# Loading the last weight of a decode step: one transfer with an outermost dimension of four, or four transfers of 32 partitions

## The chip, the cores and the metric

The kernel runs on one core of a Trainium2 chip. The metric is the device time in microseconds (us), median of the runs. A ratio is computed as the mean time of one kernel's fast runs over that of the other's of the same rounds, so it is not quite the ratio of the medians that are quoted.

## The reference

One decode step of two sequences: attention over a cache of 16384 positions and 32 heads, and beside it a small MLP, mixed by a gate. Cut to what matters:

```python
def _A_ref(x, k_cache, v_cache, wq, wo):          # B=2, H=32, Sk=16384, Dh=128, D=1024
    q = ...                                       # x @ wq, by heads
    p = softmax(einsum("bhqd,bhkd->bhqk", q, k_cache) * Dh ** -0.5)
    o = einsum("bhqk,bhkd->bhqd", p, v_cache)
    return o.transpose(0, 2, 1, 3).reshape(B, Sq, H * Dh) @ wo      # wo: 4096 x 1024, bf16
# _B_ref: layernorm, w1, w2, w3, w4 ... (cut)
return g * a + (1 - g) * b
```

K and V together are 537 MB, wo is 8.39 MB. wo is needed last, once the attention output of every head is there.

## The kernel before

K and V tiles of 8.39 MB (128 partitions x 64 KB) stream through three large buffers. wo takes such a buffer too, so its load is issued when the buffer of the last K tile is free. At that moment the last V tile is still in flight. SP issues all transfers.

```python
def load_v(i):
    t = big_tile("Vn")                            # [128, 32768] bf16, one of three buffers
    nc.sync.dma_start(out=t[:].rearrange("p (j d) -> p j d", d=Dh), in_=cache_rows(A_v_cache, i))
# ... (cut)
WO_SPLIT = [16, 8, 4, 2, 1, 1]                    # rows per partition in each of six pieces

def load_wo():
    t = big_tile("wo")[:].rearrange("p (r n) -> p r n", n=D)
    src = A_wo.rearrange("(h a r) n -> a h r n", a=4, r=32)
    r0 = 0
    for n in WO_SPLIT:
        nc.sync.dma_start(out=t[:, r0 : r0 + n, :], in_=src[:, :, r0 : r0 + n, :])
        r0 += n
# ... (cut)
def wo_stage():
    Q = const.tile([P, B, 32], BF16)
    for b in range(B):
        nc.vector.transpose(out=Q[:, b, :], in_=OT[:, b, :])
    wo = wt.pop("wo").rearrange("k r (p c) -> k r p c", c=KC)
    for r in range(32):
        for c in range(KC):                       # KC = 8: 256 products in all
            nc.tensor.matmul(wo_acc[:, c, :], lhsT=wo[:, r, :, c], rhs=Q[:, :, r],
                             start=(r == 0 and c == 0), stop=(r == 31 and c == KC - 1))
```

`OT` holds dimension d of head h at partition d. VectorE transposes it in blocks of 32 x 32, so partition 32a+h of `Q` holds head h, dimensions 32a to 32a+31. Partition 32a+h of wo must therefore hold wo's rows 128h+32a+r. One step in memory cannot express that order over 128 partitions; the source has two dimensions, a (4) and h (32).

## Time and profile before

| | before |
|---|---|
| time, median of the first 3 runs | 1420.8 us (1418.2 to 1423.4) |
| span of the profiled run | 1417.6 us |
| last V tile usable | 1317.0 us |
| Q ready | 1324.8 us |
| first and last piece of wo usable | 1372.7 and 1413.8 us |
| PE waiting for wo | 73.7 us |

The slices of the page divide the span into 40 equal parts: granted TensorE clock and busy share of the DMA engines in tenths, and GB/s.

```profile
PEclk9988888687886887888885878888878787888555
DMA  9999999999999999999999999999999999999221
GB/s 413 439 423 435 439 428 429 437 426 441 428 432 432 429 438 433 424 441 437 419 443 435 424 435 435 432 432 431 439 430 429 435 437 422 441 433 394 85 89 58
```

DMA is busy all the time at about 430 GB/s, except in the last three slices, where it moves 85, 89 and 58 GB/s at two and one tenths. What is loaded there shows in the timeline (start, duration, engine, line, operation, count; in brackets the idle time before it and what ended it):

```profile
1296.17 103.53 SPq L125 DMA_DIRECT2D wo<-in_A_wo_dram  x6
...
1316.97 5.65 PE L338 MATMUL O<-Vn,PT 128*32 128x512 bf16 x64 [10.20 <-DMA Vn<-in_A_v_cache_dram]
...
1324.60 0.21 DVE L374 STREAM_TRANSPOSE Q<-OT 128x32 bf16<-128x32 bf16 x1
...
1372.70 7.86 PE L378 MATMUL wo_acc<-Q,wo 128*128 128x2 bf16 x128 [48.34 <-DMA wo<-in_A_wo_dram]
...
1393.63 4.01 PE L378 MATMUL wo_acc<-Q,wo 128*128 128x2 bf16 x64 [13.07 <-DMA wo<-in_A_wo_dram]
...
1413.81 0.65 PE L378 MATMUL wo_acc<-Q,wo 128*128 128x2 bf16 x8 [2.00 <-DMA wo<-in_A_wo_dram]
...
1414.96 0.41 SPq L523 DMA_DIRECT2D out_dram<-out_pm  x1
```

The last V product starts at 1316.97 us, Q is ready at 1324.8, and then PE stands still for 48 us until the first piece of wo is there. SP needs 103 us to get six instructions out. The waits of PE in this stretch (what waited, for what, us in total, times, longest):

```profile
PE wo_acc L378 <- DMA wo<-in_A_wo_dram: 73.7, 6, 48.3
PE O L338 <- DMA Vn<-in_A_v_cache_dram: 10.2, 1, 10.2
```

PE is not the limit: the group of all 256 products is 16.4 us of work, and 73.7 us of idle time before it (busy, mean ns of one | idle time and its cause):

```profile
L378 PE MATMUL wo_acc<-Q,wo 128*128 128x2 bf16 x256 | 16.4, 199 | 73.7 <-DMA wo<-in_A_wo_dram 73.7
```

A table of stretches (limits and length in us, busy time and count of five engines, granted clock, DMA share, GB/s) shows how many DMA engines work:

```profile
core 0: us, PE busy (x) PEld busy (x) DVE busy (x) ACT busy (x) POOL busy (x), PEclk, DMA share, GB/s
1304.00:1314.00 10.00, 0.56 (x2) 0.50 (x2) 1.27 (x5) 0.78 (x2) 0.00 (x0) 0.50 0.70 237
1314.00:1324.00 10.00, 6.33 (x70) 3.16 (x71) 0.00 (x0) 0.58 (x1) 0.00 (x0) 0.65 0.25 80
...
1334.00:1344.00 10.00, 0.00 (x0) 0.00 (x0) 0.00 (x0) 0.00 (x0) 0.00 (x0) 0.50 0.26 85
1344.00:1354.00 10.00, 0.00 (x0) 0.00 (x0) 0.00 (x0) 0.00 (x0) 0.00 (x0) 0.50 0.23 79
```

A share of 0.25 at a fifth of the usual rate is four engines of 16.

The trace also has one record for each packet that a DMA engine moved, with start, size and duration, though not with the number of the engine. The 64 KB packets at the end are rows of the last V tile, and the 128 packets of 32 KB are the rows of wo's first piece. In the kernel before, nearly all 64 KB packets took 2.42 us; the exceptions are the 11 that started from 1308.6 us on, beside the first packets of wo, and took 3.0 to 4.1 us. Of wo's 128 packets, 63 took about 1.22 us and 34 about 2.42 us. Later two of the four engines at a time appear to hinder each other: two packets that start at 1341.4 us take 2.42 us each, while those that start around them take 1.22.

### The profile page before, as it was taken

Reading aid. Unit: us, or ns where it says so; the run is one execution under the profiler, and the core shown is the slowest. Engines: PE = TensorE matmul, PEld = TensorE weight load, DVE = VectorE, ACT = ScalarE, POOL = GpSimd, SP = SyncE. Lnnn points to the kernel's source line nnn. Section 1 sums busy time; section 2 is a strip of 40 time slices with the busy share of each in tenths; the row PEclk is TensorE's granted clock in tenths of the full one; section 3 lists DMA queues with packets and bytes.
Section 4 is the critical chain, followed back from the end, with each engine's and each line's share of the span. In section 5 each row is a group of like instructions: output and inputs, shape, how many; then the busy total and the mean of one; then the engine's idle time right before and its main releaser. Section 6 shows DMA issues by size and latency. Waiting matters only on the chain.

```text
span 1417.6 us, 12917 instructions
## 1 busy us (share of the span) xinstructions
PE 827.6 (58%) x5523; PEld 400.9 (28%) x5586; DVE 707.6 (50%) x862; ACT 45.5 (3%) x100; POOL 14.4 (1%) x45
## 2 busy tenths in 40 slices
PE   2575666655667655556666556666655565566122
PEld 2232322422234222222324222222222222222022
DVE  0665566555545554555662555665655554556000
ACT  0000000000000000000000000000000000000000
POOL 0000000000000000000000000000000000000000
PEclk9988888687886887888885878888878787888555
DMA  9999999999999999999999999999999999999221
GB/s 413 439 423 435 439 428 429 437 426 441 428 432 432 429 438 433 424 441 437 419 443 435 424 435 435 432 432 431 439 430 429 435 437 422 441 433 394 85 89 58
DMA packets 11474, 573.37 MB, mean 404 GB/s; under 512 B 1816, under 2 KB 1816, under 8 KB 2200
## 3 DMA queue, kind: packets, MB, share of 16 engines
q1 hardware_dynamic: 11416, 572.54, 93.9%
q8 instruction: 44, 0.72, 0.2%
q14 instruction: 14, 0.11, 0.0%
HBM read 572.53 MB, written 0.00 MB: 404 GB/s over the span
## 4 chain that ended last, share of the span: by engine, by line
PE 25%; DVE 21%; DMA 21%; another core or an unknown queue 12%; issue 11%; SPq 7%; ACT 2%; ACTq 0%; POOL 0%
DVE T L286 18%; DMA Kn<-in_A_k_cache_dram 16%; PE S L294 13%; SPq L125 7%; PE O L338 6%; DMA wt<-in_B_w_dram 4%; PE misc L430 3%; PE misc L201 2%; PE misc L348 2%; DMA wo<-in_A_wo_dram 2%; ACT Pr L322 1%; DVE PT L326 1%; ACT Os L346 1%; DVE mx L315 1%
## 5 line engine op out<-in xcount | busy, mean ns | idle before, releaser
L294 PE MATMUL S<-T,z 128*128 128x512 bf16 x1985 | 581.3, 421 | 342.3 <-DVE T L286 321.7
L286 DVE STREAM_TRANSPOSE T<-Kn 128x1024 f32<-128x1024 f32 x512 | 612.2, 1229 | 266.8 <-DMA Kn<-in_A_k_cache_dram 218.3
L294 PEld LDWEIGHTS <-z 128*128 128x128 bf16 x2048 | 218.7, 107 | 699.4 <-issue 537.2
L338 PE MATMUL O<-Vn,PT 128*32 128x512 bf16 x2048 | 119.8, 387 | 10.2 <-DMA Vn<-in_A_v_cache_dram 10.2
L338 PEld LDWEIGHTS <-PT 128*32 128x32 bf16 x2048 | 73.1, 140 | 56.2 <-issue 16.2
L365 DVE TENSOR_TENSOR OT<-misc,rinv 128x2 bf16<-128x2 f32 x32 | 5.1, 160 | 162.1 <-PE misc L348 162.1
L201 PE MATMUL misc<-rs,ones_f 128*128 128x2 f32 x64 | 17.9, 350 | 76.5 <-DVE rs L358 76.5
L378 PE MATMUL wo_acc<-Q,wo 128*128 128x2 bf16 x256 | 16.4, 199 | 73.7 <-DMA wo<-in_A_wo_dram 73.7
L346 ACT COPY Os<-O 128x512 f32<-128x512 f32 x32 | 18.7, 585 | 1092.1 <-PE O L338 1092.1
L348 PE MATMUL misc<-osel,Os 128*128 128x2 f32 x256 | 33.7, 254 | 22.2 <-ACT Os L346 22.2
L517 DVE TENSOR_TENSOR fin<-wo_acc,g_bc 128x16 f32<-128x16 f32 x1 | 0.2, 174 | 89.7 <-PE wo_acc L378 89.7
L348 PEld LDWEIGHTS misc<-osel,Os 128*128 128x128 f32 x256 | 31.0, 191 | 36.7 <-ACT Os L346 36.7
L430 PEld LDWEIGHTS <-wt 128*128 128x128 bf16 x576 | 35.7, 171 | 18.4 <-DMA wt<-in_B_w_dram 17.1
L305 DVE TENSOR_REDUCE m<-S 128x1 f32<-128x512 f32 x32 | 22.2, 693 | 36.9 <-PE S L294 36.9
L201 PEld LDWEIGHTS misc<-rs,ones_f 128*128 128x128 f32 x64 | 16.2, 314 | 81.2 <-issue 78.5
L326 DVE STREAM_TRANSPOSE PT<-Pr 128x512 bf16<-128x512 bf16 x32 | 22.7, 711 | 28.7 <-ACT Pr L322 28.7
L378 PEld LDWEIGHTS <-wo 128*128 128x128 bf16 x256 | 15.9, 169 | 74.2 <-DMA wo<-in_A_wo_dram 74.2
L322 ACT ACTIVATE Pr<-S,nb 128x512 bf16<-128x512 f32 x32 | 22.0, 687 | 124.0 <-DVE nb L317 121.0
L201 PE MATMUL misc<-mdiag,ones_f 128*128 128x128 f32 x64 | 15.6, 325 | 15.6 <-DVE mdiag L308 15.6
L315 DVE TENSOR_REDUCE mx<-misc 64x1 f32<-64x64 f32 x64 | 14.2, 222 | 19.0 <-PE misc L201 18.6
L264 POOL TENSOR_TENSOR z<-qsel,own 128x32 bf16<-128x32 bf16 x32 | 10.8, 337 | 1225.6 <-PE S L294 1194.6
L239 PE MATMUL misc<-xT,wt 128*128 128x2 bf16 x256 | 7.1, 165 | 25.5 <-DVE xT L234 23.1
(70 smaller groups left out, 106.9 us busy)
## 6 DMA issues: line engine op xcount, KB each, us to landing
wt<-in_B_w_dram SPq DMA_DIRECT2D x2, 7168.0 KB
wt<-in_B_w_dram SPq DMA_DIRECT2D x2, 2048.0 KB, 37.6
wo<-in_A_wo_dram SPq DMA_DIRECT2D x1, 4096.0 KB
wo<-in_A_wo_dram SPq DMA_DIRECT2D x1, 2048.0 KB
wo<-in_A_wo_dram SPq DMA_DIRECT2D x1, 1024.0 KB
Kn<-in_A_k_cache_dram SPq DMA_DIRECT2D x32, 52.3
Vn<-in_A_v_cache_dram SPq DMA_DIRECT2D x32, 37.9
wo<-in_A_wo_dram SPq DMA_DIRECT2D x1, 512.0 KB
```

The source lines that it names most:

```text
L125: nc.sync.dma_start(out=t[:, r0 : r0 + n, :], in_=src[:, :, r0 : r0 + n, :])
L201: nc.tensor.matmul(ps[:], lhsT=ones_f[:], rhs=src, start=True, stop=True)
L286: nc.vector.transpose(out=T[:].rearrange("p w j s -> p j w s"), in_=Kw[:, m * CW : (m + 1) * CW].rearrange("p (j w e) -> p j w e", w=2, e=32),
L294: nc.tensor.matmul(S[:], lhsT=z[:, v, NM - 1 - m : NM - 1 - m + P], rhs=Tb[:, v // 2, :, v % 2], start=(m == 0 and v == 0), stop=(m == NM ...
L315: nc.vector.reduce_max(out=mx[pa, :], in_=mall[pa, pa], axis=AX.X)
L322: nc.scalar.activation(out=Pr[:], in_=S[:], func=ACTF.Exp, bias=nb[:], scale=scale, accum_out=rs[:])
L326: nc.vector.transpose(out=PT[:], in_=Pr[:])
L338: nc.tensor.matmul(O[32 * g : 32 * g + 32, :], lhsT=PT[:, m : CJ * 32 : 16], rhs=V[:, j0 : j0 + 4, :], start=(m == 0), stop=(m == NM - 1),)
L346: nc.scalar.copy(out=Os[:].rearrange("p x d -> p (x d)"), in_=O[:])
L348: nc.tensor.matmul(oc[:], lhsT=Os[:, x, :], rhs=osel[:, x, :], start=(x == 0), stop=(x == 3))
L378: nc.tensor.matmul(wo_acc[:, c, :], lhsT=wo[:, r, :, c], rhs=Q[:, :, r], start=(r == 0 and c == 0), stop=(r == 31 and c == KC - 1),)
L430: nc.tensor.matmul(ps[:, c, :], lhsT=w[:, r, :].rearrange("k (p c) -> k p c", c=C)[:, :, c], rhs=actT[:, r, :], start=(r == 0), stop=(r == ...
```

## The change

The intent is to get wo onto all DMA engines. Each piece becomes four transfers, one for each a, so that the outermost dimension of both sides is h, 32.

```diff
-        src = A_wo.rearrange("(h a r) n -> a h r n", a=4, r=32)
+        src = A_wo.rearrange("(h a r) n -> h a r n", a=4, r=32)
         r0 = 0
         for n in WO_SPLIT:
-            nc.sync.dma_start(out=t[:, r0 : r0 + n, :], in_=src[:, :, r0 : r0 + n, :])
+            for a in range(4):
+                nc.sync.dma_start(
+                    out=t[32 * a : 32 * a + 32, r0 : r0 + n, :], in_=src[:, a, r0 : r0 + n, :]
+                )
             r0 += n
```

## The prediction

> **What bounds the kernel.** Over the slices of the span DMA is 9 tenths busy at about 430 GB/s until about 1310 us: the caches are streamed and DMA is the limit. The last three slices show DMA at 2, 2 and 1 tenths and 85, 89, 58 GB/s: only wo (8.39 MB) is still loading. In the chain of waits the end is wo's transfers, not arithmetic: PE waits 73.7 us for wo in six waits (groups of instructions). By the timeline the last V tile is usable at 1316.97 us, its product is reduced by 1324.8, then PE idles to 1372.7 for wo's first piece; last piece usable 1413.81, output issued 1414.96, span end 1417.6. So the tail is about 97 us after V, some 89 of them exposed.
>
> **Why it is slow.** 88/430 of the rate and a DMA share of 0.25 mean four of 16 DMA engines. That agrees with the Trainium skill, "DMA: Bandwidth & Descriptors", section "Why a DMA increments its semaphore by 16 and not by 1": the engine count is the largest number up to 16 that divides both sides' outermost dimension, here 4 (source outermost "a").
>
> **What changes.** 24 transfers of 32 partitions replace 6 of 128. Nothing changes on PE, DVE, ACT, POOL but which semaphores PE awaits. Outermost is now 32, so 16 engines. Issue costs 18 more SP instructions at about 0.35-0.5 us, from 1296 us on, behind 20 us of V traffic: hidden.
>
> But 32 partitions do not reach all SBUF ports. The Trainium skill, "SBUF — State Buffer", section "Door 1: The DMA port swizzle", gives 8 of 16 ports for partitions 0-31 and the same for 0-63. So the 16 engines would share 8 ports in pairs, first through a=0,1 (even ports), then a=2,3 (odd ports). The trace of before shows the cost of sharing: of wo's 128 packets of 32 KB, 63 took about 1.22 us and 34 about 2.42 us, twice as much, the others between. I expect mostly 2.4 us: about half rate, 215 GB/s.
>
> **Sum.** wo starts on the late engines when V finishes, 1315-1317. Full rate: 8.39 MB / 430 = 19.5 us, landing 1336; then PE limits: 256 weight loads at 61 ns = 15.7 us after the first piece (landing 1326), end 1342.5. Half rate: 39 us, less a little where paired engines run out of step (their V endings differ by 0.1-0.4 us): last piece usable about 1353-1355, plus 0.7 us matmul and 3.1 us to the end: span 1357-1359. Measured time sits about 2 to 3 us above span. Saving about 60 us; 75 if ports didn't matter.
>
> Predicted 1360 us, range 1347 to 1368; faster by over 2%: 0.97; within 2%: 0.025; slower: 0.005.
>
> **What would show it.** (1) DMA share in the tail about 0.9-1.0 while moving only 200-250 GB/s. (2) wo packets of 32 KB mostly at 2.4 us. (3) PE's idle time for wo about 20-25 us instead of 74: first piece usable near 1335, then each later piece still waited for. (4) V's landing and everything before 1316 unchanged within 2 us. (5) SP's issues no longer blocked for tens of us (before: 54.9 us for one).
>
> **What would make it wrong.** If paired engines are well out of step (the trace shows V ending on seven engines about 9 us before the rest), or the pairs are formed across these two groups, the ports are shared little, wo arrives at nearly full rate and PE's 15.7 us limit the end: about 1347. If wo on the early engines collides with V's last writes to the odd ports, V lands some us later. If small transfers (64 KB each at the end) cost a fixed time each that does not overlap, the end comes some us later, 1365 or more.

## The result, and the profile after

The change makes the kernel faster: 1366.0 us (1364.6 to 1366.7, 4 runs) against 1420.3 us (1418.2 to 1423.4, 4 runs), a ratio of 0.9615 with a 95% interval of 0.9595 to 0.9634. The saving is 54.3 us; about 60 had been forecast.

| | before | after | forecast for after |
|---|---|---|---|
| span of the profiled run | 1417.6 | 1364.4 | 1357 to 1359 |
| last V tile usable | 1317.0 | 1326.7 | 1316 to 1317 |
| first piece of wo usable | 1372.7 | 1345.4 | near 1335 |
| PE waiting for wo | 73.7 | 11.4 | 20 to 25 |
| end of the last wo product | 1414.5 | 1361.5 | about 1355 |
| 32 KB packets of wo, mean | 1.67 | 2.48 | mostly 2.4 |
| 64 KB packets of V that started after 1304 us: how many, mean | 28, 2.92 | 28, 4.91 | unchanged |

The same slices of the page, for the changed kernel:

```profile
PEclk9988887688885888777778677888777788887766
DMA  9999999999999999999999999999999999999995
GB/s 400 439 442 431 429 431 423 437 431 439 429 437 431 431 435 437 431 429 429 429 433 444 431 431 433 429 431 435 437 429 429 433 431 437 441 431 430 431 255 139
```

The DMA engines are now at nine tenths down to the last slice but one, yet in the last two they move 255 and 139 GB/s. The stretches show it without the mixing of the slices:

```profile
1304.00:1314.00 10.00, 0.87 (x4) 0.62 (x4) 1.65 (x6) 0.78 (x2) 0.00 (x0) 0.64 1.01 220
1314.00:1324.00 10.00, 0.00 (x0) 0.00 (x0) 0.00 (x0) 0.00 (x0) 0.00 (x0) 0.50 0.99 202
1324.00:1334.00 10.00, 6.58 (x72) 3.42 (x72) 0.00 (x0) 0.59 (x1) 0.00 (x0) 0.67 1.00 206
1334.00:1344.00 10.00, 0.04 (x1) 0.00 (x0) 0.37 (x2) 0.00 (x0) 0.00 (x0) 0.67 0.68 152
1344.00:1354.00 10.00, 8.22 (x134) 8.22 (x135) 0.00 (x0) 0.00 (x0) 0.00 (x0) 0.50 0.66 177
```

From 1304 to 1334 us the DMA share is 1.0 and the rate 202 to 220 GB/s. All engines are occupied and carry half of what they carry elsewhere in this kernel. That rate includes the last V tile: from the moment when the first engines turn from V to wo (1304.2 us), V's packets on the others take 4.9 us instead of 2.42.

The timeline shows what follows from it:

```profile
1296.92 61.25 SPq L127 DMA_DIRECT2D wo<-in_A_wo_dram  x24
...
1326.73 5.56 PE L342 MATMUL O<-Vn,PT 128*32 128x512 bf16 x64 [19.22 <-DMA Vn<-in_A_v_cache_dram]
...
1334.27 0.21 DVE L378 STREAM_TRANSPOSE Q<-OT 128x32 bf16<-128x32 bf16 x1
...
1345.40 7.64 PE L382 MATMUL wo_acc<-Q,wo 128*128 128x2 bf16 x125 [11.37 <-DMA wo<-in_A_wo_dram]
1353.42 8.06 PE L382 MATMUL wo_acc<-Q,wo 128*128 128x2 bf16 x131 [0.38 <-issue]
...
1361.99 0.41 SPq L527 DMA_DIRECT2D out_dram<-out_pm  x1
```

V is usable 9.8 us later than before. Its last packet ends at 1325.2 us. The first piece of wo is 128 packets, eight for each of 16 engines; by an estimate the engine that was last with V needs 8 x 2.48 = 19.8 us more for its share, which gives 1345.0. The piece was usable at 1345.4. PE waits for wo only once, for the first piece, and then runs through its 256 products without another wait (the gap at 1353 us is one of issue):

```profile
PE O L342 <- DMA Vn<-in_A_v_cache_dram: 19.2, 1, 19.2
PE wo_acc L382 <- DMA wo<-in_A_wo_dram: 11.4, 1, 11.4
...
PE wo_acc L382 <- issue: 0.4, 1, 0.4
```

SP, which was to be free, waits in a new way:

```profile
SPq L127 <- DMA Vn<-in_A_v_cache_dram: 26.6, 1, 26.6
SPq L127 <- DMA wo<-in_A_wo_dram: 24.6, 12, 4.6
```

SP issues seven transfers between 1296.9 and 1300.0 us. The eighth waits 26.6 us until V lands, and twelve later ones wait for an earlier piece of wo. The compiled program gives every transfer one of eight completion counters in turn, and an issue has to wait until the earlier transfer on its counter has landed. Six transfers never ran into this; 24 do. The four transfers of the first piece are among the seven that were issued without such a wait.

### The profile page after: what moved, and what is told of

It is laid out like the page before. It is cut to its first block, busy times and chain, and to the rows that moved or that the text cites. A ratio compares the mean times of both kernels' runs of the same rounds, so it can differ in the third digit from the quotient of the medians.

```text
span 1364.4 us, 12947 instructions
## 1 busy us (share of the span) xinstructions
PE 829.0 (61%) x5523; PEld 401.0 (29%) x5586; DVE 707.2 (52%) x862; ACT 45.6 (3%) x100; POOL 14.5 (1%) x45
## 4 chain that ended last, share of the span: by engine, by line
PE 28%; DVE 23%; DMA 20%; another core or an unknown queue 13%; issue 13%; ACT 2%; SPq 0%; ACTq 0%; POOL 0%
DVE T L290 19%; DMA Kn<-in_A_k_cache_dram 16%; PE S L298 14%; PE O L342 7%; DMA wo<-in_A_wo_dram 3%; PE misc L434 3%; PE misc L352 2%; PE misc L205 2%; ACT Pr L326 1%; DVE PT L330 1%; PE wo_acc L382 1%; ACT Os L350 1%; DVE mx L319 1%; DVE mdiag L312 1%
## 5 line engine op out<-in xcount | busy, mean ns | idle before, releaser
L205 PEld LDWEIGHTS misc<-rs,ones_f 128*128 128x128 f32 x64 | 16.1, 312 | 81.2 <-issue 78.4
L382 PE MATMUL wo_acc<-Q,wo 128*128 128x2 bf16 x256 | 15.7, 198 | 11.7 <-DMA wo<-in_A_wo_dram 11.4
L434 PE MATMUL misc<-xn2T,wt 128*128 128x2 bf16 x224 | 14.4, 202 | 9.1 <-DMA wt<-in_B_w_dram 9.1
```

The source lines that it names most:

```text
L205: nc.tensor.matmul(ps[:], lhsT=ones_f[:], rhs=src, start=True, stop=True)
L434: nc.tensor.matmul(ps[:, c, :], lhsT=w[:, r, :].rearrange("k (p c) -> k p c", c=C)[:, :, c], rhs=actT[:, r, :], start=(r == 0), stop=(r == ...
```

## The experiments

Nine kernels were run. All theories below concern where the half rate comes from, why V is late, and what sets the end. One warning on the word correct: the comparison with the reference is coarse for wo, because the attention branch adds little to the output. For the kernels that permute wo, correctness rests on the index arithmetic given with them.

### Is it the memory side? pitch64k and kcache256k

In the changed kernel 16 engines at once read rows of wo that lie 256 KB apart. The Trainium skill, "DMA: Bandwidth & Descriptors", section "Latency and other measured facts", lists row pitches at large powers of two that slow a copy, from 512 KiB (207 GB/s against 214) up, so this was a rival to the ports. Two kernels separate the two sides. Their outputs are wrong, which doesn't matter for the times.

pitch64k: destinations as in the changed kernel, rows 64 KB apart.

```diff
-        src = A_wo.rearrange("(h a r) n -> h a r n", a=4, r=32)
+        src = A_wo.rearrange("(a h r) n -> h a r n", a=4, r=32)
```

> Wrong result on purpose: the destinations stay four groups of 32 partitions, but a partition's rows are read 64 KB apart in memory (as the K and V tiles are) instead of 256 KB. Theory P (32 partitions reach only half of the SBUF ports): nothing changes, wo's 32 KB packets stay at 2.4 to 2.6 us, V is usable at about 1326 us, time 1366 +- 4. Rival H (sixteen engines reading rows 256 KB apart collide in memory): packets fall to about 1.2 us, V usable at about 1317, time about 1348.

kcache256k: 128 partitions wide, rows 256 KB apart.

```diff
-        src = A_wo.rearrange("(h a r) n -> h a r n", a=4, r=32)
+        src = A_k_cache.rearrange("b h (x y) d -> (b h x) (y d)", y=1024)
...
-            for a in range(4):
-                ...
+            nc.sync.dma_start(out=t[:, r0 : r0 + n, :],
+                in_=src[0:P, r0 * D : (r0 + n) * D].rearrange("p (r n) -> p r n", n=D))
```

> Wrong result on purpose: six transfers of 128 partitions, as wide as those of K and V, but read from the K cache with rows 256 KB apart, the pitch that wo's rows have in the changed kernel. Theory P: full rate, 32 KB packets about 1.2 us, V usable at 1317, time about 1348. Rival H: packets about 2.4 us, V late as in the changed kernel, time 1358 to 1368.

Measured (one run each, state unknown): pitch64k 1366.3 us, 32 KB packets 2.49 us in the mean, V usable at 1327.0 us. kcache256k 1345.8 us, all 128 packets of 32 KB between 1.1 and 1.3 us, mean 1.217, V usable at 1315.7 us. The pitch of 256 KB costs nothing and the pitch of 64 KB cures nothing. The cause is on the side of the destination, or in the shape of the transfer.

### Neighbouring partitions, or transfers of 32 rows? stride4

The 24 transfers and their source rows stay; transfer a goes to partitions a, a+4, a+8 and so on. Then wo's rows 128h+32a+r lie in partition 4h+a, so Q's partitions must move from 32a+h to 4h+a. A 128 x 128 permutation (an identity with rearranged columns) does it with one matmul and one copy. (The table that the expectation speaks of is the one that the prediction names, in "SBUF — State Buffer", section "Door 1: The DMA port swizzle".)

```diff
-                    out=t[32 * a : 32 * a + 32, r0 : r0 + n, :], in_=src[:, a, r0 : r0 + n, :]
+                    out=t[a:P:4, r0 : r0 + n, :], in_=src[:, a, r0 : r0 + n, :]
...
+    perm = const.tile([P, P], BF16, name="perm")
+    nc.vector.tensor_copy(out=perm[:].rearrange("p (h a) -> p h a", a=4),
+                          in_=ident_f[:].rearrange("p (a h) -> p h a", a=4))
...
+        Qp_ps = misc_psum([P, B, 32])
+        nc.tensor.matmul(Qp_ps[:], lhsT=perm[:], rhs=Q[:], start=True, stop=True)
+        Q = const.tile([P, B, 32], BF16, name="Qp")
+        nc.vector.tensor_copy(out=Q[:], in_=Qp_ps[:])
```

> The changed kernel's 24 transfers of 32 partitions with the same source rows, but transfer a goes to partitions a, a+4, a+8, ... which touch all 16 ports of the Trainium skill's table (Q's partitions are permuted to match, as in perm128). Theory P (a block of 32 neighbouring partitions reaches 8 ports): packets of 32 KB average below 2.0 us instead of 2.48, V usable before 1324, time 1347 to 1361. Rival W (any transfer of 32 rows, two per engine, is slow wherever it lands): packets 2.4 to 2.6 us and 1366 +- 3.

Measured: 1357.8 us (1357.6 to 1357.8, 4 runs), ratio to before 0.9563 (0.9549 to 0.9577). All 128 packets of 32 KB took about 1.22 us, mean 1.216, and all 28 late V packets stayed under 4 us. The first two stretches, to be set beside those of the changed kernel:

```profile
1304.00:1314.00 10.00, 0.78 (x4) 0.53 (x3) 1.65 (x6) 0.78 (x2) 0.00 (x0) 0.60 0.98 420
1314.00:1324.00 10.00, 6.89 (x73) 3.46 (x73) 0.59 (x3) 0.59 (x1) 0.00 (x0) 0.72 0.84 346
```

V is usable at 1315.62 us again. Nothing but the partitions of the destination differs in the transfers, so the blocks of 32 neighbouring partitions are the cause of the half rate and of V's delay. (Which engine meets which at which port is not shown by this.) The time does not follow fully, for a reason that has nothing to do with DMA:

```profile
1315.62 5.65 PE L348 MATMUL O<-Vn,PT 128*32 128x512 bf16 x64 [8.21 <-DMA Vn<-in_A_v_cache_dram]
...
1323.74 0.23 DVE L388 CAST Qp<-misc 128x64 bf16<-128x64 f32 x1 [0.28 <-PE misc L386]
...
1337.62 15.51 PE L392 MATMUL wo_acc<-Qp,wo 128*128 128x2 bf16 x256 [13.92 <-DMA wo<-in_A_wo_dram]
```

Q is ready at 1324.0, and PE waits until 1337.6. In the compiled program the first weight load of wo waits for all eight counters: the framework does not tell the strided destinations apart and makes the first product wait for the last transfer (landed at 1337.4), though the four transfers of the first piece had landed at 1325.3. The changed kernel's first product waits for its own four transfers only.

### Does width alone help? width64

Two transfers per piece, each of 64 neighbouring partitions, with wo in partition order 4h+a (consecutive rows, Q permuted as in stride4).

```diff
+        src = A_wo.rearrange("(p r) n -> p r n", p=P)
...
+            for p0 in (0, 64):
+                nc.sync.dma_start(out=t[p0 : p0 + 64, r0 : r0 + n, :],
+                                  in_=src[p0 : p0 + 64, r0 : r0 + n, :])
```

> Two transfers of 64 neighbouring partitions per piece instead of four of 32, rows consecutive (perm128's layout), four rows per engine and transfer. Theory P: 64 neighbours reach the same 8 ports as 32 do, so 32 KB packets stay near 2.4 us, V late (about 1325), time 1360 to 1367. Rival W (number of rows per engine in a transfer): half way to perm128's full rate, packets about 1.8 us, time about 1355.

Measured (one run, state unknown): 1365.9 us; 32 KB packets 2.48 us in the mean, all 28 late V packets above 4 us. Sixty-four neighbours are as slow as 32.

### Which ports meet V's? order2301

```diff
-            for a in range(4):
+            for a in (2, 3, 0, 1):
```

> The changed kernel with the four transfers of a piece issued in the order a = 2, 3, 0, 1. Under P in its simple form V's late half writes the ports that a = 0, 1 share, so starting at a = 2, 3 lets V land at 1317 instead of 1326.7 and saves 5 to 10 us: 1356 to 1361. If V's delay isn't a matter of which ports meet (H, or a limit on all transfers together), V stays at about 1326 and the time at 1366 +- 3.

Measured: 1365.9 us (1365.6 to 1366.6, 4 runs), ratio 0.9619 (0.9603 to 0.9635), no different from the changed kernel. V stays late:

```profile
1325.82 5.52 PE L342 MATMUL O<-Vn,PT 128*32 128x512 bf16 x64 [18.41 <-DMA Vn<-in_A_v_cache_dram]
```

All 28 late V packets took more than 4 us (mean 4.87), with either order. The simple picture, in which V suffers only while wo writes V's own half of the ports, is refuted.

### What does V's delay cost? after_v

wo is held until the last V tile has landed: a copy of a few bytes out of that tile into the part that wo then overwrites comes first.

```diff
+        nc.sync.dma_start(
+            out=t[:, 15:32, 0:16],
+            in_=vn_tiles[NT - 1][:, 0:272].rearrange("p (r n) -> p r n", n=16),
+        )
```

> The changed kernel, but wo may start only when the last V tile has landed: a copy of a few bytes from that V tile into the part that wo overwrites goes first (about 3 us by itself). If the transfers of wo are what delays V: V usable at 1316 instead of 1326.7, wo starts on all engines at about 1319, first piece 1338 to 1341, last piece 1357 to 1361 and waited for by PE piece after piece, time 1362 to 1368. If V's delay has another cause: V stays at about 1326 and the time becomes 1372 or more.

Measured: 1367.7 us (1367.2 to 1368.0, 4 runs), ratio 0.9632 (0.9616 to 0.9648).

```profile
1315.54 6.41 PE L346 MATMUL O<-Vn,PT 128*32 128x512 bf16 x64 [8.70 <-DMA Vn<-in_A_v_cache_dram]
...
1318.60 41.34 SPq L131 DMA_DIRECT2D wo<-in_A_wo_dram  x24
...
1341.21 7.65 PE L386 MATMUL wo_acc<-Q,wo 128*128 128x2 bf16 x125 [17.51 <-DMA wo<-in_A_wo_dram]
...
1356.85 3.73 PE L386 MATMUL wo_acc<-Q,wo 128*128 128x2 bf16 x56 [0.71 <-DMA wo<-in_A_wo_dram]
...
1361.70 0.60 PE L386 MATMUL wo_acc<-Q,wo 128*128 128x2 bf16 x8 [1.13 <-DMA wo<-in_A_wo_dram]
```

V is usable at 1315.5, so wo's transfers are what delays it in the changed kernel. But the total is no better. wo's first packet starts at 1319.6 us and its last piece is used at 1361.7: 42 us, where the prediction had put 39 at most. The 32 KB packets took 2.51 us in the mean, and all of wo's packets together add up to 38.8 us for each of 16 engines, so the rate was the predicted one. The rest lies at the end: until 1357 us the engines were busy almost without a gap, and from there to the last packet (1361.0) they were idle for 2.4 of 4 us. In that time the last small transfers landed, the smallest of 64 KB; SP had to wait for earlier landings and issued the last four of them between 1357.2 and 1359.9 us.

```profile
SPq L131 <- DMA wo<-in_A_wo_dram: 30.7, 12, 4.7
```

How much of the idle time is due to these waits, and how much to the small transfers themselves, is not separated. PE now waits for later pieces too, as the prediction had described. Holding wo cost about 3 us (SP issues wo 3.0 us after V is usable). By an estimate, without the hold this kernel would stand at about 1364.7 us, 1.3 us from the changed kernel: what V loses by the overlap, wo has mostly gained by its early start.

### Do SP's new waits cost anything? split3

```diff
-    WO_SPLIT = [16, 8, 4, 2, 1, 1]
+    WO_SPLIT = [16, 8, 8]
```

> The changed kernel with three pieces of 16, 8 and 8 rows (12 transfers) instead of six pieces (24): SP then waits for an earlier landing before 5 of its issues and not before 17. If those waits of SP cost nothing because the first piece and PE's 16 us bound the end: V 1326, first piece 1345, PE end 1361 to 1363, time 1366 +- 2. If they cost: 1362 or less.

Measured (one run, state unknown): 1368.4 us, slightly above the range that was expected for free waits.

```profile
1345.12 7.66 PE L382 MATMUL wo_acc<-Q,wo 128*128 128x2 bf16 x125 [11.06 <-DMA wo<-in_A_wo_dram]
1353.14 4.24 PE L382 MATMUL wo_acc<-Q,wo 128*128 128x2 bf16 x67 [0.37 <-issue]
...
1359.38 3.98 PE L382 MATMUL wo_acc<-Q,wo 128*128 128x2 bf16 x64 [2.00 <-DMA wo<-in_A_wo_dram]
```

With 12 transfers SP waits before five issues and not before 13, and the first piece is usable at 1345.1 us all the same. The end is later because the last piece is larger: PE waits 2.0 us for it and then has 4.0 us left. The first piece was not earlier and PE started no sooner. That could hardly be otherwise: in both kernels the four transfers of the first piece are issued before SP's first wait. So SP's waits did not hold up the start that sets the end. What they cost the later pieces is hidden in the changed kernel, where PE is the later one, and the larger last piece blurs the comparison of the totals; in after_v above, where PE waits for the last pieces, they may well have cost time.

### All ports and all engines: perm128 and perm128s

perm128 loads wo as it lies in memory, 128 partitions wide, and permutes Q as in stride4.

```diff
-        src = A_wo.rearrange("(h a r) n -> h a r n", a=4, r=32)
+        src = A_wo.rearrange("(p r) n -> p r n", p=P)
         r0 = 0
         for n in WO_SPLIT:
-            for a in range(4):
-                ...
+            nc.sync.dma_start(out=t[:, r0 : r0 + n, :], in_=src[:, r0 : r0 + n, :])
             r0 += n
```

> Right result by another route: wo as six transfers of 128 partitions of consecutive rows (partition 4h+a instead of 32a+h), and Q's partitions permuted to match by one 128x128 matmul and one copy, about 1 us. All theories: 32 KB packets about 1.2 us, V usable at 1317 us, first piece of wo about 1327, then PE's 16 us for 256 products bound the end: span about 1346, time about 1348, 18 us faster than the changed kernel and 72 us faster than before.

Measured: 1345.8 us (1345.6 to 1347.0, 4 runs), ratio 0.9479 (0.9465 to 0.9493). Packets of 32 KB 1.217 us in the mean; V is usable at 1315.6 us.

```profile
1315.63 5.55 PE L345 MATMUL O<-Vn,PT 128*32 128x512 bf16 x64 [8.29 <-DMA Vn<-in_A_v_cache_dram]
...
1323.65 0.23 DVE L385 CAST Qp<-misc 128x64 bf16<-128x64 f32 x1 [0.28 <-PE misc L383]
...
1325.39 15.54 PE L389 MATMUL wo_acc<-Qp,wo 128*128 128x2 bf16 x256 [1.78 <-DMA wo<-in_A_wo_dram]
```

PE starts 1.5 us after Q is ready and doesn't wait again. The sum made for the changed kernel holds here too, at the full rate: the last V packet ends at 1315.1 us, eight packets of 1.217 us make 9.7, together 1324.9 by this estimate, and the first piece was usable at 1325.4. Of the 20 us between the two kernels, V's delay is thus one half and the half rate of the first piece the other. perm128s cuts the first piece in two:

```diff
-    WO_SPLIT = [16, 8, 4, 2, 1, 1]
+    WO_SPLIT = [8, 8, 8, 4, 2, 1, 1]
```

> perm128 with its first piece of 16 rows cut into two of 8. In perm128 PE starts on wo at 1325.4 us, 1.5 us after the permuted Q is ready (1323.9), and then never waits. With 8 rows first it can start when Q is ready: 1.5 us earlier, time about 1344.3 against 1345.8. If the time stays at 1345.8, something else holds PE's start.

Measured: 1344.0 us (1343.7 to 1345.0, 5 runs), ratio 0.9465 (0.9449 to 0.9480).

```profile
1323.52 15.48 PE L389 MATMUL wo_acc<-Qp,wo 128*128 128x2 bf16 x256 [0.32 <-DVE Qp L385]
```

PE now starts as soon as Q is copied. By the medians this is 1.8 us faster than perm128, from another set of rounds, so that step is seen in the trace rather than proven by an interval. perm128s takes 22 us less than the changed kernel. Its tail is bounded by PE's 256 small products, 15.5 us.

## Why the prediction was right or wrong

The time (1366.0) lies inside the range (1347 to 1368), near its upper end.

- **Four engines before, sixteen after: right.** The DMA share was 0.25 in the tail before and is 1.0 from 1304 to 1334 us after. That agrees with the Trainium skill, "DMA: Bandwidth & Descriptors", section "Why a DMA increments its semaphore by 16 and not by 1".
- **Half rate: right, and shown to come from the blocks of neighbouring partitions.** Share 1.0 at 202 to 220 GB/s, packets at 2.48 us instead of 1.22. pitch64k and kcache256k exclude the memory side, stride4 excludes the number and size of the transfers, width64 agrees with the equal reach of 32 and 64 neighbours in the table of "SBUF — State Buffer", section "Door 1: The DMA port swizzle".
- **"The 16 engines would share 8 ports in pairs": not shown.** In the changed kernel between 1306 and 1319 us the records have seven packets of wo and nine of V in flight, so only seven engines carried wo. All the same, each of wo's 32 KB packets that started then took 2.1 to 2.6 us. Seven engines can't all be paired among themselves, and V's packets on the other nine were slowed as well. The predicted rate was right; the picture of two wo engines at one port does not explain it alone.
- **"Half rate: 39 us, less a little where paired engines run out of step": the rate right, the end mis-sized.** This term can be read in after_v, which has the overlap with V taken away and so is the case that the prediction added up. The packets took 38.8 us per engine: the 39 of the prediction, with nothing gained by engines out of step. But from wo's first packet to its last use 42 us passed, because the engines were idle for 2.4 us between the last small transfers, and 0.7 us more lay between the last packet and its use. The prediction had named a cost of the small transfers as a risk and put nothing in the sum for it. In the changed kernel itself this did not count: the last transfer had landed at 1359.7, and PE was still busy until 1361.5 with products whose weights were there.
- **"(4) V's landing and everything before 1316 unchanged within 2 us": wrong.** V came 9.8 us later. The prediction had named a collision as a risk, and only for V's odd ports; order2301 showed that it comes with either half. The cost was nearly repaid by wo's earlier start (estimate from after_v: about 1.3 us net).
- **"(3) PE's idle time for wo about 20-25 us ... first piece usable near 1335, then each later piece still waited for": wrong.** V's last engines turn to wo only after V's delay, so the first piece came at 1345.4. By then Q had been ready for 11 us, and the rest of wo arrived during PE's 16.1 us. The end is the first piece plus PE's work: 1345.4 + 16.1 = 1361.5, and 2.9 us to the end of the span. So the total came close partly by luck, from two errors that offset each other: the first piece came about 10 us too late, but from there to the end of the last product it took 16.1 us and not the 20 of the forecast (1335 to 1355). What is left is the 6.5 us by which that end was missed.
- **"(5) SP's issues no longer blocked for tens of us": wrong.** SP waits 26.6 us once, for another reason than before. In the changed kernel PE never waited for a piece that they delayed. In after_v, where SP waits 30.7 us in twelve such waits and PE does wait for the last pieces, they probably cost part of the 2.4 us above; no run separates it.

Open is how the slow blocks slow V down. The records carry no engine number, so it cannot be read which engines and ports meet. Few engines suffice: in the kernel before, three packets of wo were in flight beside nine of V at 1309 to 1312 us, and all V packets that started from 1308.6 on were slowed. The Trainium skill, "DMA: Bandwidth & Descriptors", section "Back-pressure in remote DMA", describes stalled writes that hold up other DMA engines on the same path, for another kind of transfer. That would fit a V slowed by both halves, but no run here tests it.

## What to carry to other kernels

When a few DMA engines carry the tail of a kernel, look at two things separately: how many engines a transfer gets, from the outermost dimension of both sides, and which partitions it writes. A DMA share near 1.0 at half of the usual GB/s was the mark of the second here, and packet durations that doubled at equal size confirmed it. Rather than cut a transfer into blocks of partitions to satisfy a layout, keep it 128 partitions wide and move the permutation to the small operand (here one matmul and one copy for a 128 x 64 tile), and check what is still in flight when the new transfer starts.

## What the Trainium skill lacked or had wrong

- "SBUF — State Buffer", section "Can I just issue two DMAs to hit both halves?", gives one transfer spanning all 128 partitions as the only way to hit all 16 ports. It need not fill them: in stride4 transfers of 32 partitions, four apart, moved 32 KB packets in 1.216 us, as transfers of 128 partitions did (1.217). The section doesn't mention such a step.
- The same page, section "Door 1", has the half rate of neighbours right (2.48 us a packet for 32 and for 64), but no page says of loads from memory that such a transfer also slows others in flight (the section on back-pressure speaks of transfers between cores): all 28 packets of a 128-partition load from memory took 4.9 us instead of 2.42, whichever half of the partitions the block wrote.
- "DMA: Bandwidth & Descriptors", section "Latency and other measured facts", starts its list of row pitches at 512 KiB. At 256 KB, 128 rows at a time, there is no loss on a load (1.217 us per 32 KB packet in kcache256k).
